# A decode-attention kernel: the last V tile is loaded in five pieces and multiplied slot by slot into small accumulators

## The chip, the cores and the metric

The kernel runs on one core of one Trainium2 chip. The metric is the time of one execution on the device, in microseconds (us). Executions of one kernel that belong together agree within about 0.3%, so a difference of less than one per cent needs several runs of both kernels on the same chip. "Before" and "after" are the two kernels.

Names used throughout: PE is the matmul engine, PEld its weight loads, DVE the vector engine, ACT the scalar engine, SP the engine that issues most loads. A "landing" is the moment at which the semaphore of a load is complete.

## The reference, cut to what matters

One query token attends to 65,536 keys: 32 query heads in 8 groups, one key/value head per group, head size 128.

```python
B, Hq, Hkv, Sq, Sk, D = 1, 32, 8, 1, 65536, 128      # bf16
k = jnp.repeat(k, Hq // Hkv, axis=1)                  # 4 query heads share a K/V head
v = jnp.repeat(v, Hq // Hkv, axis=1)
scores = jnp.einsum("bhqd,bhkd->bhqk", q, k) * D ** -0.5
p = softmax(scores, axis=-1)
return jnp.einsum("bhqk,bhkd->bhqd", p, v)
```

K and V together are 268 MB and each byte is used once, so the least that any kernel can do is to read them.

## The kernel before

K and V of a group are each read as four tiles of 4 MB (128 partitions of 32 KB; 128 "slots" of 128 values on each partition). Loads go through five buffers, one load for each tile. K tiles of group g+1 alternate with V tiles of group g, so the last four loads of the program are V tiles of group 7.

```python
def load(view, name):
    t = iopool.tile([P, T * D], bf16, name=name, tag="io")      # T = 128 slots, D = 128
    nc.sync.dma_start(out=t[:, :], in_=view)
    return t
# ... k_step: scores of a K tile into S;  softmax: S -> E (bf16 weights of V) and rl (1/sum)

def v_step(g, j):                                   # V tile j of group g
    vt = load(v_view[g, j], "vt")
    if j == 0:
        A_tiles[g] = psa.tile([P, 2, HI * D], fp32, name="A")   # two PSUM banks
    A, E = A_tiles[g], E_tiles[g]
    vt_v = vt[:, :].rearrange("p (u i c d) -> p u c i d", u=2, i=HI, c=CW)
    for c0 in range(0, CW, NQ):
        for u in range(2):
            for s in range(NQ):                     # four groups of 32 output partitions
                c = c0 + s
                nc.tensor.matmul(out=A[s * QP:(s + 1) * QP, u, :],
                    lhsT=E[:, j, c, :], rhs=vt_v[:, u, c, :, :],
                    start=(j == 0 and c0 == 0), stop=(j == NQ - 1 and c0 == CW - NQ))

def finish(g):
    A = A_tiles.pop(g)
    As = apool.tile([P, 2, HI, D], fp32, name="As")
    nc.scalar.copy(out=As[:, 0, :, :].rearrange("p i d -> p (i d)"), in_=A[:, 0, :])
    nc.vector.tensor_copy(out=As[:, 1, :, :].rearrange("p i d -> p (i d)"), in_=A[:, 1, :])
    ps_f = psm.tile([HPG, D], fp32, name="ps_f", tag="misc")
    for i in range(NI):                             # 8 matmuls select the useful blocks of As
        nc.tensor.matmul(out=ps_f[:, :], lhsT=sel[:, i * HPG:(i + 1) * HPG],
            rhs=As[:, i // HI, i % HI, :], start=(i == 0), stop=(i == NI - 1))
    o = stats.tile([HPG, D], bf16, name="o")
    nc.vector.tensor_scalar_mul(out=o[:, :], in0=ps_f[:, :], scalar1=rl_tiles.pop(g)[:, :])
    nc.scalar.dma_start(out=out[0, g * HPG:(g + 1) * HPG, 0, :], in_=o[:, :])
# ... cut
```

A matmul of `v_step` multiplies 32 columns of weights by 512 columns of V, of which only a block diagonal is wanted. That saves instructions; `finish` picks the wanted blocks, copied to `As`, with the 8 matmuls of `ps_f`. In the profile these are 16 passes, since an fp32 matmul shows as two.

Of the kernel before, what the change touches and what calls it, by code (L numbers as in the profile page):

```python
# [12 lines left out]
fp32 = mybir.dt.float32  # L13
# [5 lines left out]
def kernel(  # L19
# [19 lines left out]
    nc = tc.nc  # L39
    P = nc.NUM_PARTITIONS  # L40
    B, Hq, Sq, D = q.shape
    _, Hkv, Sk, _ = k.shape
    HPG = Hq // Hkv
    assert B == 1 and Sq == 1 and D == P and HPG == 4 and Hq == 32
    NQ = 4
    QP = 32
    T = Sk // (NQ * NQ * QP)
    NI = QP // HPG
    CW = T // NI
# [9 lines left out]
    apool = ctx.enter_context(tc.tile_pool(name="apool", bufs=1))  # L59
    stats = ctx.enter_context(tc.tile_pool(name="stats", bufs=2))  # L60
    pss = ctx.enter_context(tc.tile_pool(name="pss", bufs=1, space=bass.MemoryType.PSUM))
    psa = ctx.enter_context(tc.tile_pool(name="psa", bufs=1, space=bass.MemoryType.PSUM))
    psm = ctx.enter_context(tc.tile_pool(name="psm", bufs=2, space=bass.MemoryType.PSUM))

    k_view = k[0].rearrange("g (j p t) d -> g j p (t d)", j=NQ, p=P)
    v_view = v[0].rearrange("g (j p t) d -> g j p (t d)", j=NQ, p=P)

    def load(view, name):
        t = iopool.tile([P, T * D], bf16, name=name, tag="io")
        nc.sync.dma_start(out=t[:, :], in_=view)  # L70
        return t

    q4 = const.tile([P, D], bf16)
# [4 lines left out]
    for g in range(Hkv):  # L78
# [9 lines left out]
        out=sel[:, :], in_=ident[:, :].rearrange("p (s c) -> p c s", s=NQ),  # L88
        axis=AX.X, op=ALU.add,
    )  # L90
    selh = const.tile([P, HPG], fp32)
    nc.vector.tensor_reduce(
        out=selh[:, :], in_=sel[:, :].rearrange("p (i h) -> p h i", h=HPG),
# [11 lines left out]
    for a in range(NQ):  # L105
        r = slice(a * QP, (a + 1) * QP)
        z0 = QP - HPG + a * QP
        for b in range(2):
            for e in range(2):
                nc.vector.tensor_copy(  # L110
                    out=Z[r, b, e, :, z0:z0 + HPG], in_=qT_v[r, b, e, :, :]
# [3 lines left out]
    E_tiles = {}  # L115
    rl_tiles = {}
    A_tiles = {}

    def k_step(g, j):
        kt = load(k_view[g, j], "kt")  # L120
        if j == 0:
            S_tiles[g] = pss.tile([P, NQ, 512], fp32, name="S")
        S = S_tiles[g]
        for i in range(NI):
            kT = ktp.tile([P, CW * D], bf16, name="kT")
            nc.vector.transpose(  # L126
                out=kT[:, :].bitcast(i32),
                in_=kt[:, i * CW * D:(i + 1) * CW * D].bitcast(i32),
            )
            kT_v = kT[:, :].rearrange("q (c b p e) -> q b e c p", b=2, p=QP, e=2)  # L130
            for be in range(4):
                b, e = be // 2, be % 2
                w0 = QP - HPG - i * HPG
                nc.tensor.matmul(  # L134
                    out=S[:, j, :NCOL],
                    lhsT=Z[:, b, e, g, w0:w0 + P],
                    rhs=kT_v[:, b, e, :, :],
                    start=(i == 0 and be == 0),
                    stop=(i == NI - 1 and be == 3),
                )  # L140

    def softmax(g):
        S = S_tiles.pop(g)
        mx = stats.tile([P, 1], fp32, name="mx")
        nc.vector.reduce_max(out=mx[:, :], in_=S[:, :, :NCOL], axis=AX.XY)  # L145
        ps_t = psm.tile([1, P], fp32, name="ps_t", tag="misc")
        nc.tensor.transpose(out=ps_t[:, :], in_=mx[:, :], identity=ident[:, :])  # L147
        m4 = stats.tile([1, HPG], fp32, name="m4")
        nc.vector.tensor_reduce(
            out=m4[:, :], in_=ps_t[:, :].rearrange("o (r h) -> o h r", h=HPG),  # L150
            axis=AX.X, op=ALU.max,
        )
        mrow = stats.tile([1, P], fp32, name="mrow")
        nc.vector.tensor_scalar_mul(  # L154
            out=mrow[:, :].rearrange("o (r h) -> o r h", h=HPG),
            in0=m4[:, None, :].to_broadcast([1, P // HPG, HPG]),
            scalar1=-SCALE,
        )
        ps_b = psm.tile([P, 1], fp32, name="ps_b", tag="misc")
        nc.tensor.matmul(out=ps_b[:, :], lhsT=mrow[:, :], rhs=one[:, :], start=True, stop=True)  # L160
        nm = stats.tile([P, 1], fp32, name="nm")
        nc.vector.tensor_copy(out=nm[:, :], in_=ps_b[:, :])  # L162
        ET = etp.tile([P, NQ * NCOL], bf16, name="ET")
        ls = stats.tile([P, 1], fp32, name="ls")
        nc.scalar.activation(  # L165
            out=ET[:, :].rearrange("p (a n) -> p a n", a=NQ), in_=S[:, :, :NCOL],
            func=ACT.Exp, bias=nm[:, :], scale=SCALE, accum_out=ls[:, :],
        )
        E = epool.tile([P, NQ, CW, QP], bf16, name="E")
        nc.vector.transpose(out=E[:, :, :, :].rearrange("p a c r -> p (a c r)"), in_=ET[:, :])  # L170
        E_tiles[g] = E
        ps_l = psm.tile([HPG, 1], fp32, name="ps_l", tag="misc")
        nc.tensor.matmul(out=ps_l[:, :], lhsT=selh[:, :], rhs=ls[:, :], start=True, stop=True)  # L173
        rl = stats.tile([HPG, 1], fp32, name="rl")
        nc.vector.reciprocal(out=rl[:, :], in_=ps_l[:, :])
        rl_tiles[g] = rl

    HI = NI // 2

    def v_step(g, j):  # L180
        vt = load(v_view[g, j], "vt")
        if j == 0:
            A_tiles[g] = psa.tile([P, 2, HI * D], fp32, name="A")
        A = A_tiles[g]
        E = E_tiles[g]
        vt_v = vt[:, :].rearrange("p (u i c d) -> p u c i d", u=2, i=HI, c=CW)
        for c0 in range(0, CW, NQ):
            for u in range(2):
                for s in range(NQ):
                    c = c0 + s  # L190
                    nc.tensor.matmul(  # L191
                        out=A[s * QP:(s + 1) * QP, u, :],
                        lhsT=E[:, j, c, :],
                        rhs=vt_v[:, u, c, :, :],
                        start=(j == 0 and c0 == 0),
                        stop=(j == NQ - 1 and c0 == CW - NQ),
                    )

    def finish(g):
        A = A_tiles.pop(g)  # L200
        E_tiles.pop(g)
        As = apool.tile([P, 2, HI, D], fp32, name="As")
        nc.scalar.copy(out=As[:, 0, :, :].rearrange("p i d -> p (i d)"), in_=A[:, 0, :])  # L203
        nc.vector.tensor_copy(out=As[:, 1, :, :].rearrange("p i d -> p (i d)"), in_=A[:, 1, :])  # L204
        ps_f = psm.tile([HPG, D], fp32, name="ps_f", tag="misc")
        for i in range(NI):
            nc.tensor.matmul(  # L207
                out=ps_f[:, :], lhsT=sel[:, i * HPG:(i + 1) * HPG],
                rhs=As[:, i // HI, i % HI, :],
                start=(i == 0), stop=(i == NI - 1),  # L210
            )
        o = stats.tile([HPG, D], bf16, name="o")
        nc.vector.tensor_scalar_mul(out=o[:, :], in0=ps_f[:, :], scalar1=rl_tiles.pop(g)[:, :])  # L213
        nc.scalar.dma_start(out=out[0, g * HPG:(g + 1) * HPG, 0, :], in_=o[:, :])

    for kind, g, s in seq:
        if kind == "k":
            k_step(g, s)
            if s == NQ - 1:
                softmax(g)  # L220
        else:
            v_step(g, s)
            if s == NQ - 1:
                finish(g)


# [28 lines left out]
```

## Time and profile before

| | before |
|---|---|
| time, median of the first 3 runs | 640.2 us (639.99 to 642.45) |
| read from HBM | 268.5 MB, 420 GB/s over the span of 638.6 us |
| PE, DVE busy | 61%, 54% |
| last landing to the scaling that makes `o` | 629.46 to 635.75: 6.29 us |
| scaling to the end (store, closing drain) | 635.75 to 638.58: 2.83 us |

These are two lines of the page of before. The digits are tenths, one for each of 40 equal slices of the span: the clock that PE was granted, and the busy share of the 16 DMA engines.

```profile
PEclk9998888877688776777767887668886779877767
DMA  8999999999999999999999999999999999999991
```

The reader is to see that the loads never pause until the last slice. Only what follows the last landing counts. The chain of waits of before shows that part in order of time (columns: start, duration, what).

```profile
589.55 39.91 DMA vt<-in_v_dram
629.46 0.04 issue
629.50 3.58 PE A L191 x32
...
633.16 0.59 ACT As L203
633.75 0.04 issue
633.80 1.92 PE ps_f L207 x16
635.72 0.02 issue
635.75 0.34 DVE o L213
```

The 32 matmuls of the last tile, the copies of A and the collecting passes stand one behind another. Windows of before cut this stretch by stage (columns: window; its length; busy time and number of instructions of PE, PEld, DVE, ACT and POOL; granted PE clock; DMA share; GB/s).

```profile
616.00:623.00 7.00, 3.20 (x32) 1.31 (x32) 0.00 (x0) 0.00 (x0) 0.00 (x0) 0.53 0.99 426
623.00:629.46 6.46, 0.09 (x4) 0.00 (x0) 0.00 (x0) 0.00 (x0) 0.00 (x0) 0.74 0.43 183
629.50:633.10 3.60, 3.55 (x32) 1.21 (x31) 0.00 (x0) 0.00 (x0) 0.00 (x0) 0.53 0.00 0
633.80:635.80 2.00, 1.91 (x16) 1.30 (x16) 0.72 (x2) 0.00 (x0) 0.00 (x0) 1.00 0.00 0
```

The clock was 0.53 while the last tile was multiplied and 1.00 while it was collected. The DMA share fell to 0.43 well before the landing, because the 16 engines do not end together: the 16 increments of this load's semaphore come between 624.70 and 629.46.

### The profile page before, as it was taken

Reading aid. Unit: us, or ns where it says so; the run is one execution under the profiler, and the core shown is the slowest. Engines: PE = TensorE matmul, PEld = TensorE weight load, DVE = VectorE, ACT = ScalarE, POOL = GpSimd, SP = SyncE. Lnnn points to the kernel's source line nnn. Section 1 sums busy time; section 2 is a strip of 40 time slices with the busy share of each in tenths; the row PEclk is TensorE's granted clock in tenths of the full one; section 3 lists DMA queues with packets and bytes.
Section 4 is the critical chain, followed back from the end, with each engine's and each line's share of the span. In section 5 each row is a group of like instructions: output and inputs, shape, how many; then the busy total and the mean of one; then the engine's idle time right before and its main releaser. Section 6 shows DMA issues by size and latency. Waiting matters only on the chain.

```text
span 638.6 us, 5252 instructions
## 1 busy us (share of the span) xinstructions
PE 390.7 (61%) x2216; PEld 154.6 (24%) x2216; DVE 343.5 (54%) x340; ACT 21.7 (3%) x25; POOL 4.9 (1%) x7
## 2 busy tenths in 40 slices
PE   0695945776447864487644776547666465775533
PEld 0232312232113321133211232213222122222211
DVE  0999833775336754366553655545555564455300
ACT  0000000000001000010000100001000010000100
POOL 3000000000000000000000000000000000000000
PEclk9998888877688776777767887668886779877767
DMA  8999999999999999999999999999999999999991
GB/s 367 445 434 428 427 426 431 442 431 428 432 426 429 431 436 431 430 433 428 427 431 432 431 433 435 428 427 430 433 431 433 433 430 429 432 431 430 427 436 82
DMA packets 9494, 268.80 MB, mean 421 GB/s; under 512 B 1280, under 2 KB 1280, under 8 KB 1280
## 3 DMA queue, kind: packets, MB, share of 16 engines
q1 hardware_dynamic: 9216, 268.44, 97.8%
q8 instruction: 17, 0.28, 0.2%
q10 hardware_dynamic: 256, 0.04, 0.0%
q14 instruction: 5, 0.04, 0.0%
HBM read 268.47 MB, written 0.01 MB: 420 GB/s over the span
## 4 chain that ended last, share of the span: by engine, by line
DMA 55%; PE 19%; DVE 16%; issue 8%; ACT 2%; ACTq 0%; DVEq 0%
DMA kt<-in_k_dram 46%; PE S L134 13%; DVE kT L126 10%; DMA vt<-in_v_dram 6%; PE A L191 4%; DMA q_85<-in_q_dram 2%; DVE E L170 2%; DVE mx L145 2%; PE ps_f L207 2%; ACT ET L165 2%; DVE As L204 1%; PE ps_b L160 0%; DVE o L213 0%; DVE Z L110 0%; PE ps_t L147 0%
## 5 line engine op out<-in xcount | busy, mean ns | idle before, releaser
L134 PE MATMUL S<-kT,Z 128*128 128x512 bf16 x1024 | 288.5, 441 | 187.5 <-DVE kT L126 184.0
L126 DVE STREAM_TRANSPOSE kT<-kt 128x1024 int32<-128x1024 int32 x256 | 292.2, 1205 | 191.5 <-DMA kt<-in_k_dram 190.9
L134 PEld LDWEIGHTS <-Z 128*128 128x128 bf16 x1024 | 110.3, 108 | 364.5 <-issue 285.0
L191 PE MATMUL A<-vt,E 128*32 128x512 bf16 x1024 | 76.7, 431 | 18.0 <-DMA vt<-in_v_dram 17.9
L191 PEld LDWEIGHTS <-E 128*32 128x32 bf16 x1024 | 28.4, 104 | 57.1 <-issue 40.2
L165 ACT ACTIVATE ET<-S,nm 128x2048 bf16<-128x2048 f32 x8 | 15.7, 1967 | 573.2 <-DVE nm L162 573.2
L207 PE MATMUL ps_f<-As,sel 128*4 128x128 f32 x128 | 22.2, 334 | 12.1 <-DVE As L204 9.4
L170 DVE STREAM_TRANSPOSE E<-ET 128x2048 bf16<-128x2048 bf16 x8 | 18.5, 2311 | 16.3 <-ACT ET L165 16.3
L145 DVE TENSOR_REDUCE mx<-S 128x1 f32<-128x2048 f32 x8 | 18.3, 2291 | 12.6 <-PE S L134 12.6
L204 DVE COPY As<-A 128x512 f32<-128x512 f32 x8 | 5.3, 663 | 31.8 <-ACT As L203 31.8
L207 PEld LDWEIGHTS ps_f<-As,sel 128*4 128x4 f32 x128 | 11.6, 100 | 20.7 <-DVE As L204 11.6
L147 PE MATMUL ps_t<-ident,mx 128*1 128x128 f32 x8 | 2.3, 286 | 16.9 <-DVE mx L145 16.9
L213 DVE TENSOR_SCALAR o<-ps_f,rl 4x128 bf16<-4x128 f32 x8 | 2.7, 338 | 14.1 <-PE ps_f L207 14.1
L100 DVE STREAM_TRANSPOSE qT<-q_85 128x64 int32<-128x64 int32 x1 | 0.2, 245 | 16.1 <-DMA q_85<-in_q_dram 16.1
L173 PE MATMUL ps_l<-ls,selh 128*4 128x1 f32 x16 | 1.5, 165 | 8.2 <-ACT ET L165 8.2
L203 ACT COPY As<-A 128x512 f32<-128x512 f32 x8 | 4.6, 576 | 36.0 <-PE A L191 36.0
L147 PEld LDWEIGHTS ps_t<-ident,mx 128*1 128x1 f32 x8 | 0.6, 79 | 19.5 <-DVE mx L145 16.5
L160 PE MATMUL ps_b<-one,mrow 1*128 1x1 f32 x16 | 3.8, 306 | 2.2 <-DVE mrow L154 2.2
L160 PEld LDWEIGHTS ps_b<-one,mrow 1*128 1x128 f32 x16 | 3.2, 245 | 6.6 <-DVE mrow L154 6.6
L162 DVE COPY nm<-ps_b 128x1 f32<-128x1 f32 x8 | 1.2, 151 | 6.3 <-PE ps_b L160 6.3
L104 POOL MEMSET Z<- 128x4992 bf16 x1 | 4.3, 4262 | 0.0
L173 PEld LDWEIGHTS ps_l<-ls,selh 128*4 128x4 f32 x16 | 0.7, 84 | 12.4 <-ACT ET L165 12.4
(29 smaller groups left out, 10.8 us busy)
## 6 DMA issues: line engine op xcount, KB each, us to landing
kt<-in_k_dram SPq DMA_DIRECT2D x32, 4096.0 KB, 45.4
vt<-in_v_dram SPq DMA_DIRECT2D x32, 4096.0 KB, 39.4
out_dram<-o ACTq DMA_DIRECT2D x8, 1.0 KB
q_85<-in_q_dram ACTq DMA_DIRECT2D x4, 8.0 KB, 6.2
```

The source lines that it names most:

```text
L104: nc.gpsimd.memset(Z[:, :, :, :, :], 0.0)
L126: nc.vector.transpose(out=kT[:, :].bitcast(i32), in_=kt[:, i * CW * D:(i + 1) * CW * D].bitcast(i32),)
L134: nc.tensor.matmul(out=S[:, j, :NCOL], lhsT=Z[:, b, e, g, w0:w0 + P], rhs=kT_v[:, b, e, :, :], start=(i == 0 and be == 0), stop=(i == NI - ...
L145: nc.vector.reduce_max(out=mx[:, :], in_=S[:, :, :NCOL], axis=AX.XY)
L147: nc.tensor.transpose(out=ps_t[:, :], in_=mx[:, :], identity=ident[:, :])
L160: nc.tensor.matmul(out=ps_b[:, :], lhsT=mrow[:, :], rhs=one[:, :], start=True, stop=True)
L165: nc.scalar.activation(out=ET[:, :].rearrange("p (a n) -> p a n", a=NQ), in_=S[:, :, :NCOL], func=ACT.Exp, bias=nm[:, :], scale=SCALE, acc ...
L170: nc.vector.transpose(out=E[:, :, :, :].rearrange("p a c r -> p (a c r)"), in_=ET[:, :])
L191: nc.tensor.matmul(out=A[s * QP:(s + 1) * QP, u, :], lhsT=E[:, j, c, :], rhs=vt_v[:, u, c, :, :], start=(j == 0 and c0 == 0), stop=(j == N ...
L203: nc.scalar.copy(out=As[:, 0, :, :].rearrange("p i d -> p (i d)"), in_=A[:, 0, :])
L204: nc.vector.tensor_copy(out=As[:, 1, :, :].rearrange("p i d -> p (i d)"), in_=A[:, 1, :])
L207: nc.tensor.matmul(out=ps_f[:, :], lhsT=sel[:, i * HPG:(i + 1) * HPG], rhs=As[:, i // HI, i % HI, :], start=(i == 0), stop=(i == NI - 1),)
```

## The change

The intent is to shorten the part behind the last landing. The last tile is loaded in five pieces of 64, 32, 16, 8 and 8 slots. The large accumulators then close one tile earlier and are copied and collected while the last tile loads. The slots of the last tile are multiplied one by one, each only by its own 4 columns of weights, so nothing has to be picked afterwards: 120 slots in turn into four groups of 4 rows of a small accumulator `Dp`, the last 8 straight into `ps_f`. A last matmul adds the sum of the four groups. In passing, A and As become two tiles each in all groups, and the last store is issued from SP.

```diff
-    def load(view, name):
+    def load(view, name, cuts=()):
         t = iopool.tile([P, T * D], bf16, name=name, tag="io")
-        nc.sync.dma_start(out=t[:, :], in_=view)
+        edges = [0, *cuts, T]
+        for lo, hi in zip(edges, edges[1:]):
+            nc.sync.dma_start(out=t[:, lo * D:hi * D], in_=view[:, lo * D:hi * D])
...
+    last_a = NQ - 2
+    CUTS = (T // 2, 3 * T // 4, 7 * T // 8, T - T // 16)
+    EDGE = CUTS[-1]
...                      (v_step: A is two tiles A0, A1; group 7 stops at tile last_a)
-    def finish(g):
+    def collect(g, stop):
...                      (as finish, with As in two tiles; returns ps_f, left open if not stop)
+    def last_step(g, j):
+        vt = load(v_view[g, j], "vt", CUTS)
+        E = E_tiles.pop(g)
+        Dp = psm.tile([P, D], fp32, name="Dp", tag="misc")
+        nc.vector.memset(Dp[:, :], 0.0)
+        def slot(t, dst, start, stop):
+            i, c = t // CW, t % CW
+            nc.tensor.matmul(
+                out=dst, lhsT=E[:, j, c, i * HPG:(i + 1) * HPG],
+                rhs=vt[:, t * D:(t + 1) * D], start=start, stop=stop,
+            )
+        ps_f = collect(g, False)
+        for t in range(EDGE):
+            s = t % NQ
+            slot(t, Dp[s * QP:s * QP + HPG, :], t < NQ, t >= EDGE - NQ)
+        Ds = stats.tile([P, D], fp32, name="Ds")
+        nc.vector.tensor_copy(out=Ds[:, :], in_=Dp[:, :])
+        for t in range(EDGE, T):
+            slot(t, ps_f[:, :], False, False)
+        nc.tensor.matmul(
+            out=ps_f[:, :], lhsT=selh[:, :], rhs=Ds[:, :], start=False, stop=True
+        )
+        store(g, ps_f, nc.sync)
```

More of the change, by code (lines that the diff above doesn't have):

```diff
@@ L182, in v_step @@
         if j == 0:
-            A_tiles[g] = psa.tile([P, 2, HI * D], fp32, name="A")
+            A_tiles[g] = [
+                psa.tile([P, HI * D], fp32, name=f"A{u}") for u in range(2)
+            ]
         A = A_tiles[g]
         E = E_tiles[g]
+        end = NQ - 1 if g < Hkv - 1 else last_a
         vt_v = vt[:, :].rearrange("p (u i c d) -> p u c i d", u=2, i=HI, c=CW)
@@ L191, in v_step @@
                     nc.tensor.matmul(
-                        out=A[s * QP:(s + 1) * QP, u, :],
+                        out=A[u][s * QP:(s + 1) * QP, :],
                         lhsT=E[:, j, c, :],
@@ L195, in v_step @@
                         start=(j == 0 and c0 == 0),
-                        stop=(j == NQ - 1 and c0 == CW - NQ),
+                        stop=(j == end and c0 == CW - NQ),
                     )
-    def finish(g):
+    def collect(g, stop):
         A = A_tiles.pop(g)
-        E_tiles.pop(g)
-        As = apool.tile([P, 2, HI, D], fp32, name="As")
-        nc.scalar.copy(out=As[:, 0, :, :].rearrange("p i d -> p (i d)"), in_=A[:, 0, :])
-        nc.vector.tensor_copy(out=As[:, 1, :, :].rearrange("p i d -> p (i d)"), in_=A[:, 1, :])
+        As = [apool.tile([P, HI, D], fp32, name=f"As{u}") for u in range(2)]
+        nc.scalar.copy(out=As[0][:, :, :].rearrange("p i d -> p (i d)"), in_=A[0][:, :])
+        nc.vector.tensor_copy(out=As[1][:, :, :].rearrange("p i d -> p (i d)"), in_=A[1][:, :])
         ps_f = psm.tile([HPG, D], fp32, name="ps_f", tag="misc")
@@ L208, in finish, with store @@
                 out=ps_f[:, :], lhsT=sel[:, i * HPG:(i + 1) * HPG],
-                rhs=As[:, i // HI, i % HI, :],
-                start=(i == 0), stop=(i == NI - 1),
-            )
+                rhs=As[i // HI][:, i % HI, :],
+                start=(i == 0), stop=(stop and i == NI - 1),
+            )
+        return ps_f
+    def store(g, ps_f, dma):
         o = stats.tile([HPG, D], bf16, name="o")
         nc.vector.tensor_scalar_mul(out=o[:, :], in0=ps_f[:, :], scalar1=rl_tiles.pop(g)[:, :])
-        nc.scalar.dma_start(out=out[0, g * HPG:(g + 1) * HPG, 0, :], in_=o[:, :])
+        dma.dma_start(out=out[0, g * HPG:(g + 1) * HPG, 0, :], in_=o[:, :])
+    def last_step(g, j):
[21 more added lines that the diff above has]
+        store(g, ps_f, nc.sync)
     for kind, g, s in seq:
@@ L221 @@
         else:
-            v_step(g, s)
-            if s == NQ - 1:
-                finish(g)
+            if g == Hkv - 1 and s == NQ - 1:
+                last_step(g, s)
+            else:
+                v_step(g, s)
+                if s == NQ - 1:
+                    store(g, collect(g, True), nc.scalar)
 _INS = ['q', 'k', 'v']
```

## The prediction

> **What bounds the kernel now.** The loads. The page gives 268 MB at 420 GB/s over 638.6 us; the DMA engines are 0.9 busy up to the last of 40 slices, PE 61% and DVE 54%. It is a stream of 64 loads of 4 MB (about 9.7 us each), then a tail without loads. Only the tail changes. From the timeline and the chain of waits: the last V tile lands at 629.46; 32 matmuls into A to 633.08; ACT copies half of A to 633.75; DVE the other half only after ACT (633.78, 0.69 us); 16 passes of ps_f 633.80 to 635.72; scaling 0.34; the store and the closing drain to 638.6. Tail after the landing: 9.1 us, of which 2.5 us (store, drain) stays.
>
> **What the last load looks like.** The windows of 1 us show the DMA share fall from 1.06 (623-624) to 0.46 (624-626) and 0.16 (627-628). The packet records say why: of the 16 engines seven are done at 624.3-624.9, seven at 627.4-627.8, one at 628.4, the last at 629.05, each with eight 32 KB packets of 1.215 us for the tile. The Trainium skill, "DMA: Bandwidth & Descriptors", section on why a DMA increments its semaphore by 16, says that each engine posts its own increment and only all 16 mean landed; the trace agrees (16 increments, 624.70 to 629.46). So every piece waits for the slowest engine.
>
> **Landings after (estimates from its 9.72 us a tile plus 0.4 us to the increment).** Slots 0-63 at 624.6, to 95 at 627.1, to 111 at 628.4, to 119 at 629.1, the last at 629.8. I add 0.3 us for 32 more packets per engine: 256-byte packets took 15-18 ns where their bytes at the 32 KB rate need 9.5.
>
> **PE after.** The large accumulators close with V tile 2: its landing 619.8, matmuls to 623.1, both copies now side by side (separate tiles) to 623.9, ps_f to 625.6, all under the load. Slots start there. A slot is a 4-column weight load and a 128-column matmul, in rotating groups. Four groups run together in the trace (the next four 427 ns later for 512 columns, or 215 ns at full clock), so 128 columns allow 14-27 ns a slot; the tightest stretch of PE issues one instruction per 23 ns, 46 ns a slot. At 40 ns, slots 0-119 done near 630.4. The last 8 share one group, one after another: about 0.1 us each, as the ps_f passes (109 ns): 631.2. The closing matmul and its drain 0.5: scaling starts at 631.8 instead of 635.75.
>
> **Sum.** Removed 3.6 + 0.7 + 1.9 = 6.2 us after the landing; added 0.3 (packets) + 0.6 (slots left behind) + 0.8 + 0.5 = 2.2. Gain near 4 us at 40 ns a slot, under 2 at 60. I discount to 3.2 us, as one more instruction fetch (17 of 16 KB, each stalling an engine about 1 us) may hit the slowest engine. Earlier groups' parallel copies save nothing, under the load.
>
> Predicted 637.0 us, 80% range 635.0 to 639.3; faster by over 2% 0.01, within 2% 0.98, slower 0.01.
>
> **To check.** Last landing within 1 us of 629.5; A's ps_f passes before 626; slot starts 25-60 ns apart; 1.5 to 2.5 us from last landing to scaling.
>
> **What would make it wrong.** Small pieces load much slower (2 KB runs); slots at 100 ns each, so the gain vanishes; pieces issued late because of a wait on the queue.

## The result, and the profile after

| | before | after |
|---|---|---|
| median of 6 runs each | 640.3 us (639.99 to 642.45) | 635.41 us (635.2 to 635.73) |
| ratio | | 0.9915, 95% interval 0.9899 to 0.9931 |
| span of the profile | 638.6 us | 633.7 us |
| last landing | 629.46 | 630.14 |
| last landing to the scaling | 6.29 us | 0.91 us |
| scaling to the end | 2.83 us | 2.67 us |

Ratios are computed as the mean time of one kernel's fast runs over that of the other's of the same rounds, so they are not quite the ratio of the medians: 0.9915 of 640.2 us is 634.8, the median is 635.41. The mean of before is pulled up by two runs at 642.2 and 642.45. The second of them was among the three runs that the prediction had, and it took no notice of it.

The direction and the place of the gain were right, the size was too small: 3.2 us were predicted, and the medians are 4.9 us apart, the means 5.5. This is the chain of waits of after for the same stretch.

```profile
600.07 30.08 DMA vt<-in_v_dram
630.14 0.04 issue
630.19 0.61 PE ps_f L238 x8
630.79 0.23 PE ps_f L251 x2
631.02 0.03 issue
631.05 0.34 DVE o L225
```

Nothing is left behind the landing but the last eight slots and the closing matmul. Lines of the timeline of after, PE and the copies only (columns: start, duration, engine, line, operation, number; in brackets the idle time before and its releaser), show what went under the load.

```profile
623.52 0.59 ACT L212 COPY As_3087<-A_2977 128x512 f32<-128x512 f32 x1 [24.37 <-PE A_2977 L200]
...
624.16 1.29 PE L216 MATMUL ps_f<-As_3087,sel 128*4 128x128 f32 x8 [0.31 <-ACT As_3087 L212]
...
626.06 1.16 PE L238 MATMUL Dp<-vt,E 128*4 128x128 bf16 x58
627.62 0.62 PE L238 MATMUL Dp<-vt,E 128*4 128x128 bf16 x32 [0.41 <-DMA vt<-in_v_dram]
...
628.88 0.40 PE L238 MATMUL Dp<-vt,E 128*4 128x128 bf16 x16 [0.63 <-DMA vt<-in_v_dram]
...
629.55 0.28 PE L238 MATMUL Dp<-vt,E 128*4 128x128 bf16 x8 [0.28 <-DMA vt<-in_v_dram]
```

Each batch of slots is done before the next piece lands, and PE waits for the load again each time (the brackets). The pace inside a batch, from the starts in the trace, is 16 slots in 0.223 us, 14 ns a slot. The windows of after answer to those of before.

```profile
616.00:623.80 7.80, 3.56 (x32) 1.21 (x31) 0.00 (x0) 0.28 (x1) 0.00 (x0) 0.50 0.95 402
623.80:626.30 2.50, 2.19 (x41) 1.62 (x38) 0.69 (x1) 0.31 (x1) 0.00 (x0) 0.82 0.79 316
626.30:630.14 3.84, 2.21 (x112) 1.65 (x107) 0.26 (x1) 0.00 (x0) 0.00 (x0) 1.00 0.32 122
630.14:631.05 0.91, 0.82 (x10) 0.53 (x9) 0.03 (x1) 0.00 (x0) 0.00 (x0) 1.00 0.00 0
```

In this profile the clock is full when the last piece lands. In before it was half at that moment.

The sum closes on the profiles: 0.69 us later landing, 5.38 us less from landing to scaling, 0.17 us less after it, together 4.86 us against 4.9 us between the spans. The interval from the landing of V tile 2 to the last one is 9.95 us with the pieces and 9.70 without, so 0.25 of the 0.69 belong to the pieces. The other 0.44 stand already at V tile 2 and are not the change's: there two profiles of one and the same kernel differ by as much (620.20 in after, 619.71 in e1).

### The profile page after: what moved, and what is told of

It is laid out like the page before. It is cut to its first block, busy times and chain, and to the rows that moved or that the text cites. A ratio compares the mean times of both kernels' runs of the same rounds, so it can differ in the third digit from the quotient of the medians.

```text
span 633.7 us, 5456 instructions
## 1 busy us (share of the span) xinstructions
PE 376.3 (59%) x2314; PEld 151.0 (24%) x2314; DVE 344.5 (54%) x342; ACT 21.7 (3%) x25; POOL 4.9 (1%) x7
## 4 chain that ended last, share of the span: by engine, by line
DMA 70%; PE 12%; DVE 9%; issue 7%; ACT 1%; ACTq 0%; DVEq 0%
DMA kt<-in_k_dram 56%; DMA vt<-in_v_dram 12%; PE S L136 8%; DVE kT L128 8%; DMA q_85<-in_q_dram 2%; DVE mx L147 1%; PE ps_f L216 1%; ACT ET L167 1%; PE A_1900 L200 0%; PE A_772 L200 0%; PE A_773 L200 0%; PE A_1901 L200 0%; DVE Z L112 0%; PE A_396 L200 0%; ACTq L77 0%
## 5 line engine op out<-in xcount | busy, mean ns | idle before, releaser
L136 PE MATMUL S<-kT,Z 128*128 128x512 bf16 x1024 | 283.9, 429 | 207.8 <-DVE kT L128 200.8
L136 PEld LDWEIGHTS <-Z 128*128 128x128 bf16 x1024 | 108.2, 106 | 381.5 <-issue 300.1
L200 PEld LDWEIGHTS <-E 128*32 128x32 bf16 x992 | 25.1, 100 | 49.4 <-issue 29.6
L200 PE MATMUL A_2977<-vt,E 128*32 128x512 bf16 x48 | 6.8, 544 | 13.6 <-DMA vt<-in_v_dram 13.6
L200 PE MATMUL A_2652<-vt,E 128*32 128x512 bf16 x64 | 8.1, 426 | 0.0
L200 PE MATMUL A_2653<-vt,E 128*32 128x512 bf16 x64 | 7.9, 421 | 0.0
L200 PE MATMUL A_397<-vt,E 128*32 128x512 bf16 x64 | 7.4, 409 | 0.0
L200 PE MATMUL A_396<-vt,E 128*32 128x512 bf16 x64 | 7.4, 401 | 0.0
L200 PE MATMUL A_2276<-vt,E 128*32 128x512 bf16 x64 | 7.0, 382 | 0.2 <-DMA vt<-in_v_dram 0.2
L200 PE MATMUL A_1148<-vt,E 128*32 128x512 bf16 x64 | 6.9, 382 | 0.0
L200 PE MATMUL A_1524<-vt,E 128*32 128x512 bf16 x64 | 6.9, 382 | 0.0
L200 PE MATMUL A_1900<-vt,E 128*32 128x512 bf16 x64 | 6.9, 382 | 0.0
L200 PE MATMUL A_772<-vt,E 128*32 128x512 bf16 x64 | 6.9, 382 | 0.0
L200 PE MATMUL A_2978<-vt,E 128*32 128x512 bf16 x48 | 6.9, 548 | 0.0
```

Source lines behind the costliest of these rows:

```text
L136: nc.tensor.matmul(out=S[:, j, :NCOL], lhsT=Z[:, b, e, g, w0:w0 + P], rhs=kT_v[:, b, e, :, :], start=(i == 0 and be == 0), stop=(i == NI - ...
L200: nc.tensor.matmul(out=A[u][s * QP:(s + 1) * QP, :], lhsT=E[:, j, c, :], rhs=vt_v[:, u, c, :, :], start=(j == 0 and c0 == 0), stop=(j == e ...
```

## The experiments

Two theories stand against each other where the gain is larger than predicted. The first: all of it lies behind the last landing, the slots run faster than the prediction took, and the clock of PE in that stretch counts as well. The rival: part of it came from elsewhere, by chance or from the parallel copies in all eight groups. Fourteen runs were made, e1 and e5 with unaltered kernels; in each the result was correct. Runs of before stood in the same rounds, 50 in all with the six of the table.

### e1: the changed kernel again

No edit. 

> The changed kernel unaltered, as the yardstick of this chip. Tail theory (all of the gain lies behind the last landing, 6.3 us before against 0.9 us after from the last landing to the scaling): 635.4 us, and before at 640.2, or near 642.3 in some runs. Rival (part of the gain is chance: two of six runs of before stood at 642.3, which no cause in the tail explains): the ratio moves clearly with the share of such runs, and the difference of the lower runs is 4.8 us, not 5.4.

Measured: 635.21 us (635.2 to 635.42), ratio 0.9903. Before, in the same rounds, 642.11 us (640.11 to 642.42). Of the 50 runs of before exactly half lie between 639.99 and 640.67 (mean 640.32), the other half between 641.99 and 642.48 (mean 642.19), and none between. After has no such second level in 11 runs (mean 635.35). So the gain is 5.0 us over the lower level of before and 6.8 over the upper, and any ratio depends on how many runs of each level it holds. The rival is right that chance is in the ratio; what makes the levels is the next question.

### e5: the kernel before again, for one more profile

No edit, one run, state unknown. 

> The kernel before, unaltered, for one more profile. It has two levels, about 640.2 and 642.2. Clock theory: at the upper level the 16 passes of the last ps_f run at half clock (213 ns apart, 3.6 us) and not at full clock (109 ns, 1.9 us) as in the profile of 640.5; at the lower level they look as there. Rival (the level comes from the loads, an engine that falls further behind): the upper level shows the last landing near 631.4 and the passes 109 ns apart.

Measured: 642.02 us, so an upper run with a profile. First its windows of the tail, then the collecting passes from its timeline:

```profile
616.00:623.00 7.00, 3.38 (x32) 1.35 (x32) 0.00 (x0) 0.00 (x0) 0.00 (x0) 0.50 1.03 445
623.00:629.30 6.30, 0.23 (x4) 0.00 (x0) 0.00 (x0) 0.00 (x0) 0.00 (x0) 0.50 0.42 182
629.30:633.00 3.70, 3.60 (x32) 1.21 (x31) 0.00 (x0) 0.00 (x0) 0.00 (x0) 0.50 0.00 0
633.60:637.30 3.70, 3.57 (x16) 1.88 (x16) 0.71 (x2) 0.01 (x1) 0.00 (x0) 0.50 0.00 0
```

```profile
633.66 3.57 PE L207 MATMUL ps_f<-As,sel 128*4 128x128 f32 x16 [0.74 <-ACT As L203]
```

The last landing is at 629.28, no later than in the lower run (629.46). The passes take 3.57 us at clock 0.50 where they took 1.91 at 1.00. That is 1.66 of the 1.71 us by which the stretch from landing to scaling is longer here (8.00 against 6.29), and the loads have no part in it. The Trainium skill, "TensorE: Matmul & The Clock Gate", section "Part 1: The HAM clock gate", says that the clock is half by default and is raised after a window of about 3.4 us of sustained matmuls, that windows run free of the kernel, and that it falls again after an idle one. The trace agrees: in the lower run the clock record changes at 605.6, 609.0, 612.4, 615.8, 622.6, 626.1 and 632.9, always by multiples of 3.4 us; in the upper run the windows fall otherwise, and from 607.5 to the end none of them raises the clock. In the lower run the window from 629.5 to 632.9 is filled with matmuls, and the clock rises at its end. In the upper run edges lie near 628.0, 631.4, 634.8 and 638.2 (an estimate: 607.51 plus multiples of 3.41 us), so each window of the tail holds a wait of PE. That the place of the windows makes the level rests on these two profiles and on the next experiment, which moves the clock by hand.

### e6 and e9: the kernel before, with PE kept at work while it waits

```diff
+    def keep_warm(vt):
+        W = psm.tile([P, 512], fp32, name="W", tag="misc")      # never read
+        for n in range(14):                                     # e9: 20
+            nc.tensor.matmul(out=W[:, :], lhsT=vt[:, 0:P], rhs=vt[:, P:P + 512],
+                start=(n == 0), stop=(n == 13))
...                      (in v_step, behind the matmuls of V tile 2 of group 7)
+        if g == Hkv - 1 and j == NQ - 2:
+            keep_warm(vt)
```

> The kernel before with 14 dummy matmuls (128 by 512, into an unread bank) between the multiplication of V tile 2 and that of tile 3, so that PE works while it would have waited for the last load. Nothing leaves the tail. Clock theory: the clock is full when the tile lands, the 32 matmuls take 2.0 us and not 3.6, the collecting passes 1.9 us always: landing to scaling 4.9 us, 638.7 us, and no run near 642. That would be 1.5 us of the gain over the lower level of before and 3.4 over the upper. If the clock doesn't matter: 640.2 and 642.2 as before.

Measured: 638.9 us (638.55 to 640.42), ratio 0.9967; four runs from 638.55 to 639.06, two above 640.1, none near 642. In the profile, of a run at 640.16, the dummies ended at 625.9 and the clock fell to half at 629.1, 0.1 us ahead of the landing. So the wait was still long enough to lose the clock, and the forecast of 638.7 us missed two of the six runs. The edit was made longer:

> As e6_before_warm with 20 dummy matmuls, not 14: there they ended 3.4 us ahead of the landing, and in the profile the clock fell to half just before it. Twenty end 1 to 2.5 us ahead. Clock theory: all runs near 638.6, from landing to scaling 4.9 us, none at 640 or 642. Rival (the runs at 638.6 of e6 had another cause): the same spread, 638.5 to 640.4.

Measured: 638.97 us, all five runs between 638.72 and 638.98. Timeline of e9:

```profile
623.86 4.85 PE L204 MATMUL W<-vt 128*128 128x512 bf16 x19 [0.33 <-issue]
...
629.62 1.91 PE L191 MATMUL A<-vt,E 128*32 128x512 bf16 x32 [0.91 <-DMA vt<-in_v_dram]
...
632.27 1.91 PE L217 MATMUL ps_f<-As,sel 128*4 128x128 f32 x16 [0.74 <-ACT As L213]
```

The same 32 matmuls that took 3.55 us take 1.91. Useless work under the load made the kernel 1.4 us faster than its lower level and 3.3 us faster than its upper one, and both levels vanished. This is the strongest run: it changes the clock and nothing else behind the landing. The clock is thus a part of what the change gains, since it also puts work on PE during the last load. What is left from e9 to after, 638.9 to 635.35, is 3.5 us, and that is work moved from behind the landing.

### e7: only the accumulators and their copies in two tiles

The changed kernel, with its last tile treated as every other one.

```diff
-        end = NQ - 1 if g < Hkv - 1 else last_a
+        end = NQ - 1
...
-            if g == Hkv - 1 and s == NQ - 1:
+            if False:
                 last_step(g, s)
```

> The large accumulators and their copies in two tiles each, in all eight groups, and nothing else of the change. Tail theory: copies of the first seven groups lie under the loads; in the last, ACT can start when its half is done, 0.3 to 0.5 us: between 0 and 0.5 us faster than before, with the two levels of before. Rival (a good part of the gain comes from parallel copies in all groups): 2 us or more faster.

Measured: 640.18 us (640.03 to 640.95), ratio 0.9985, interval 0.9968 to 1.0001. From landing to scaling the profile has 5.92 us, 0.37 less than before, as expected. The rival's 2 us are not there. One part of the forecast failed: none of six runs is at the upper level. In its profile the clock record rises at 633.6, just as the passes begin. Whether six lower runs are luck (one chance in 64, if half the runs were upper) or the earlier start of the passes helps the clock was not settled.

### e10: only the five pieces

The kernel before, its last tile loaded with the five cuts, and multiplied as before.

```diff
-        vt = load(v_view[g, j], "vt")
+        vt = load(v_view[g, j], "vt", CUTS if g == Hkv - 1 and j == NQ - 1 else ())
```

> The kernel before with its last V tile loaded in five pieces, the rest as it was: what the pieces cost by themselves. By the landings of the changed kernel (9.95 us from V tile 2 to the last piece, where one load took 9.70) the pieces cost 0.25 us; the first four matmuls can start earlier, which saves at most 0.4 us. So 640.0 to 640.5 at the lower level, 642.0 to 642.5 at the upper. If small pieces load much slower: 641 or more at the lower level and an interval from V tile 2 to the last landing above 10.5 us.

Measured: 640.33 us; three runs from 639.53 to 639.70, three from 640.96 to 641.3. The interval from V tile 2 to the last landing is 9.94 us, as expected, so small pieces load nearly as fast as one large one. The forecast of the total missed: it had the levels of before unchanged, and both are lower, by 0.7 and 1.1 us. In the profile the matmuls behind the first four begin at 628.99, half a microsecond before the last landing at 629.49, since 16 of these 28 need only the first four pieces.

### e2: the last tile in one load

```diff
-        vt = load(v_view[g, j], "vt", CUTS)
+        vt = load(v_view[g, j], "vt")
```

> The last V tile in one load; small accumulators and early collection stay. Slot theory (four column groups overlap, 14 ns a slot): 120 slots after the landing cost 1.7 us, the copy of the small accumulators and its waits about 0.6 us more, less 0.25 us for the landing that no longer carries 32 extra packets an engine: from landing to scaling 2.6 to 3.2 us, total 1.6 to 2.2 us above the changed kernel, about 637.3. With the 40 ns a slot of the prediction: 120 slots cost 4.8 us and the total is 640 or more, no better than before.

Measured: 638.53 us (636.7 to 639.36), ratio 0.9951. Timeline of its profile, a run at 639.36:

```profile
629.85 3.37 PE L238 MATMUL Dp<-vt,E 128*4 128x128 bf16 x120 [3.37 <-DMA vt<-in_v_dram]
```

The 120 slots took 3.37 us, 27 ns each, at a clock of 0.50 in the window from 629.7 to 632: again PE had been idle for 3.4 us. The forecast, made at full clock, was 1.2 us too low at the median; the fastest run, 636.7, is near it. At 40 ns a slot no run could have been that fast. So the pieces are worth about 3.2 us to this design, of which the pace of the slots at full clock explains about half.

### e3: all slots into one group of four rows

```diff
-            s = t % NQ
-            slot(t, Dp[s * QP:s * QP + HPG, :], t < NQ, t >= EDGE - NQ)
+            slot(t, Dp[0:HPG, :], t == 0, t == EDGE - 1)
```

> All 120 slots go to one group of four partitions instead of four in turn. Slot theory (the 14 ns come from the overlap of four groups): the slots run at about 55 ns, as the last eight did, 6.6 us for 120; PE then falls behind the load, ends slot 119 near 632.5 and scaling starts near 633.4, 2.3 us later than in the changed kernel: about 637.7. Rival (issue of two instructions a slot sets the pace, not the groups): the slots stay at the same pace and the time does not move from 635.4.

Measured: 637.95 us (637.64 to 638.56), 2.6 us above after. Timeline of e3:

```profile
625.88 6.86 PE L238 MATMUL Dp<-vt,E 128*4 128x128 bf16 x120
632.58 0.61 PE L238 MATMUL ps_f<-vt,E 128*4 128x128 bf16 x8
```

The slots now start every 56 ns without a pause, and scaling starts at 633.54, 2.5 us later than in after. The pace of 14 ns comes from the overlap of four groups; the issue of two instructions a slot does not limit it. The overlap is what the Trainium skill describes in "TensorE: Matmul & The Clock Gate", section "Part 3: Packing small matmuls": matmuls whose outputs lie in different strips of 32 partitions run at the same time. The trace agrees: 56 ns for one, 56 ns for four.

### e11: every slot multiplied twice

```diff
-            slot(t, Dp[s * QP:s * QP + HPG, :], t < NQ, t >= EDGE - NQ)
+            slot(t, Dp[s * QP:s * QP + HPG, :], t < NQ, False)
+            slot(t, Dp[s * QP:s * QP + HPG, :], False, t >= EDGE - NQ)
...
-        nc.vector.tensor_copy(out=Ds[:, :], in_=Dp[:, :])
+        nc.vector.tensor_scalar_mul(out=Ds[:, :], in0=Dp[:, :], scalar1=0.5)
```

> Each of the 120 slots multiplied twice, the sum halved in the copy of the small accumulators, so the result is right. Slot theory: 28 ns for a slot of the tile at full clock against 76 ns that its load takes, so all but the 8 doubled matmuls of the fourth piece stays hidden: 0 to 0.2 us above the changed kernel, 635.2 to 635.6. With the 40 ns of the prediction, 80 ns for a slot of the tile: PE would end slot 119 near 635 and the time would be 640.

Measured: 636.33 us (636.14 to 636.44), 1.0 us above after: a miss for the forecast of 0 to 0.2, and far from the 640 of a 40 ns pace. Timeline of e11:

```profile
625.53 3.18 PE L238 MATMUL Dp<-vt,E 128*4 128x128 bf16 x200
...
630.25 0.66 PE L238 MATMUL Dp<-vt,E 128*4 128x128 bf16 x33 [1.53 <-issue]
```

Two hundred matmuls in 3.18 us is the same pace of 14 to 16 ns. Then PE stood still for 1.53 us with the third and the fourth piece landed (628.28 and 628.95) and nothing that the profile shows to wait for. The record of the instruction queue has a fetch of 16 KB from 627.83 to 628.94, the 18th of the run. By its time the pause may be a wait for instructions, but this is argued and not shown: PE began again only 1.3 us after the end of that fetch, and in after a fetch from 628.78 to 630.08 stands beside no such pause. The pace of the slots stands; the price of doubling them is this pause, and its cause stays open.

### e4 and e8: collecting the large accumulators late

```diff
-        ps_f = collect(g, False)
         for t in range(EDGE):
...
+        ps_f = collect(g, False)        # e4: moved here, behind the 120 slots
```

> The 8 matmuls that collect the large accumulators (16 passes, 1.9 us) are put behind slot 119 instead of ahead of slot 0. Tail theory: they run only when the fourth piece has been multiplied, 629.7 to 631.4, and push the last eight slots: 1.2 to 1.5 us more than the changed kernel, about 636.8. If early collection were worth nothing: 635.4.

Measured: 635.32 us (635.09 to 635.66), no different from after. The run says nothing: in its timeline the collecting matmuls run ahead of the slots as before (from 623.90, the first slot at 626.15). A moved line is not a moved instruction. For e8 a dependence was added that enforces the order:

```diff
+        selw = stats.tile([P, QP], fp32, name="selw")
+        nc.vector.scalar_tensor_tensor(out=selw[:, :], in0=Ds[:, :QP], scalar=0.0,
+            in1=sel[:, :], op0=ALU.mult, op1=ALU.add)
+        ps_f = collect(g, False, selw)  # behind the copy to Ds
```

> Collection of the large accumulators behind slot 119, this time enforced: its selection matrix is made from the copy of the small accumulators (times zero, plus the old matrix), so PE cannot run it earlier; the order of the compiled instructions shows it there. Tail theory: 16 passes at full clock, 1.75 us, and the little operation on DVE, 0.2 us, move behind the last landing: scaling 1.7 to 2.2 us later than in the changed kernel, about 637.3. If early collection were worth nothing: 635.3.

Measured: 639.29 us (638.33 to 639.58), 4 us above after and not 2. In the profile the clock is 0.50 from 607.65 to 634.96 and the 16 passes take 3.57 us. So collecting early is worth what it takes away and, in this profile, the clock. That the clock stays low because PE has less to do under the load is argued and not shown.

### e12: large accumulators kept, the tile in two halves

The last tile is loaded in two pieces, the matmuls go over one accumulator and then the other, and the first is copied and collected under the second piece.

```diff
+        vt = load(v_view[g, j], "vt", (T // 2,))
+        for u in range(2):
...                      (16 matmuls into A[u]; copy A[u] to As on DVE; 4 matmuls into ps_f)
```

> A rival design without small accumulators: last tile in two halves, the half of the columns of each large accumulator that is complete is copied and collected while the second half loads. What is left behind the last landing: 16 of the 32 matmuls, one copy on DVE, 8 of the 16 passes: 2.9 us to the scaling at full clock, 4.6 at half clock, against 6.3 or 8.0 of before and 0.9 of the changed kernel. So 637.0 to 639.0. If the small accumulators and early collection were no better than this: 635.4.

Measured: 638.94 us (638.14 to 639.1), ratio 0.9964. From landing (629.44) to scaling (634.08) 4.64 us, at half clock, as expected. Small accumulators with early collection are 3.6 us better than this simpler design.

### e13: three small loads behind the last piece

```diff
+        pr = const.tile([8, D], bf16, name="pr")
+        for n in (1, 7, 8):
+            nc.sync.dma_start(out=pr[0:n, :], in_=v[0, 0, 0:n, :])
```

> The changed kernel with three small loads of 1, 7 and 8 partitions queued behind the last piece, for the times at which single engines come to the end of their queue. Theory (the instruction fetches, each beside one step back of one engine's landings, hit the same engines each time, the others never): the loads of 1 and 7 partitions land 3 us or more ahead of the last piece, that of 8 does too or has one late part. Rival (any engine may be hit): late parts among the first 7. The time doesn't matter here; it should stay within 0.5 us of 635.3.

Measured: 636.03 us, one run of unknown state, 0.7 us above after where 0.5 were allowed. The load of 7 partitions was issued only near 625.9, and that of 8 was scheduled behind the store, so they did not see the end of the queue as meant. Still, the seven parts landed at 626.6 to 626.8 (four), 628.1, 628.3 and 629.2, where the parts of the last piece landed at 625.0 to 625.6 (seven), 627.9 to 628.5 (seven), 629.0 and 629.8. So three of the seven parts of this load are late too, as the rival had it. Giving some engines a larger share of the last tile, which would have been the next version to try, has no basis in this run.

### e14: the last store from ACT

```diff
-        store(g, ps_f, nc.sync)
+        store(g, ps_f, nc.scalar)
```

> The changed kernel with its last store issued from ACT, as before, and not from SP. From the start of the scaling to the end of the span before took 2.83 us (ACT) and after 2.65 (SP): 0.2 us slower than the changed kernel, 635.5. If the issuing engine doesn't matter: 635.3.

Measured: 635.24 us (634.89 to 636.12); in the profile 2.64 us from scaling to end, after has 2.67. The issuing engine does not matter here. The 0.17 us by which this stretch was longer in the profile of before stay unexplained; over the profiles it is 2.36 (e8) to 2.94 us (e2), both stored from SP.

The profile shows something else. It is of a run at 635.78, and its clock fell to half at 629.25, before the last landing at 629.74:

```profile
629.70:632.00 2.30, 1.44 (x10) 0.93 (x9) 0.43 (x2) 0.00 (x0) 0.00 (x0) 0.50 0.00 0
```

From landing to scaling it took 1.52 us, not 0.91. So the changed tail can lose the clock too, but with so little work left there it costs 0.6 us and not 1.7.

No experiment points to a version that beats after by more than its runs scatter, so none was made. What is left behind its last landing is 0.9 us of work and 2.67 us of store and drain.

## Why the prediction was right or wrong

**Right: what bounds the kernel and where the gain lies.** The loads run as before, the change works behind the last landing, 6.2 us were said to leave it and 6.29 us stood there. The rival causes were tried alone: the split tiles take 0.4 us from this stretch (e7), the engine of the store nothing (e14).

**Right: the pieces.** 0.3 us were predicted, 0.25 measured from landing to landing (0.24 in e10). The last landing was predicted at 629.8 and came at 630.14, of which the 0.44 us that were there already at V tile 2 are scatter from run to run (in e1 the last landing is 629.66).

**Right: slots start at about 625.6** (625.84), with the collecting passes done under the load.

**Wrong, the step that failed first: "At 40 ns, slots 0-119 done near 630.4".** The prediction had the right range, 14 to 27 ns, from the overlap of four groups, and passed it over for the tightest pace of instructions seen in the trace, 23 ns each. After shows that this was no limit: it runs a matmul and a weight load in 14 ns. Measured: 13.9 ns a slot at full clock, 26.7 at half (e2), 56 in one group (e3). No slots were left behind the landing, where 0.6 us were predicted.

**Wrong: "about 0.1 us each" for the last eight.** They started every 55 ns, 0.44 us together instead of 0.8. The figure was taken from fp32 passes at full clock (109 ns); the bf16 matmuls of the same shape took half of that.

**Nearly right: the closing matmul.** 0.5 us predicted, 0.42 measured (630.63 to 631.05). From landing to scaling 2.0 us were predicted and 0.91 measured.

**Wrong, and the largest single term: the discount from 4 to 3.2 us for one more instruction fetch.** The fetch came (18 instead of 17, from 628.78 to 630.08), and it cost the load nothing that can be measured: from V tile 2 to the last landing after took 9.95 us with it, and e10, which has 17 fetches, 9.94. PE does not pause beside it either. Of the four checks, that of the last landing held; the slots started 14 ns apart and not 25 to 60, landing to scaling took 0.91 us and not 1.5 to 2.5, and the passes ended at 626.3, just past 626.

**Missing: the clock.** The windows of before showed 0.53 and 1.00 in the two halves of the tail, and the first three runs had one at 642.45. The prediction read neither. The tail of before runs at a clock that depends on where free-running windows fall: 640.3 or 642.2 us (e5), and 638.9 if PE is kept at work (e9). After has work for PE during the last load, and in its profile and that of e1 the clock was full when the last piece landed (in e14 it was not). Over the lower level the change gains 5.0 us. Of these 1.4 could be had by the clock alone; over the mean of all 50 runs of before, 641.26, it gains 5.9, of which 2.4 by the clock.

With the two sizes of slots right and without the discount, the sum of the prediction would have been 6.2 less 0.3, 0.44 and 0.5, which is 5.0 us: the gain over the lower level. So the mechanism was right and three terms were mis-sized: 0.8 us for the discount, 0.6 for slots left behind and 0.36 for the last eight. The rest, up to the 5.5 us between the means, is the runs of before at the upper level.

**Open:** why e7 had no upper run, why the stretch from scaling to end differs by 0.17 us, and which DMA engine is last. The traces hold a lead on the last: after the first 3 us of before, 22 packets of 32 KB take 1.63 us or more where the median is 1.215, and each of them starts within 0.02 us of the end of one of its 22 instruction fetches. The increments of a load lie within 0.6 us before the first fetch (42.8 us) and 1.8 us apart at 53. That the fetches part the engines is suggested by this and not shown: no run changed them.

## What to carry to other kernels

Before a stretch of small matmuls is costed, ask what limits it: matmuls in turn into four strips of 32 output partitions started every 14 ns here, where one strip took 56, and a pace read elsewhere in the trace is no bound. When an engine waits for the last load, what it does during the wait can set the clock at which it does the rest (1.4 us in e9), so read the granted clock by stage, and look at every run of before, since two levels in its times are a fact about the kernel. After an edit of the order of lines, look at the compiled order before the chip is asked.

## What the Trainium skill lacked or had wrong

- "TensorE: Matmul & The Clock Gate", section "Wait — 56ns, not 53.3ns?", gives about 25 ns as the least start-to-start time of matmuls however small they are. That is too wide: Part 3 of the same page gives about 4 ns for each further tile of a pack. Matmuls of 128 columns in rotating strips of 32 output partitions started every 14 ns on average here, each with its own weight load, 58 of them in a row in after and 200 in e11: in after bursts of four, 3 to 6 ns apart, one burst every 56 ns.
- Part 1 of the same page says that the number of slow matmuls varies from run to run with the place of the windows at the kernel's start. It does not say that a stretch behind the last load can put the runs of one kernel on two levels with nothing between: 640.32 and 642.19 us here, 25 runs each, by whether the clock rose in that stretch.
- "Runtime: NRT & Kernel Launch", section "Instruction fetch mechanics", calls the cost of crossing a 16 KiB block mostly hidden. For the last load that held (9.95 us with such a fetch in after, 9.94 without one in e10). In e11 PE paused for 1.53 us behind such a fetch (627.83 to 628.94); whether the fetch was the cause is not shown. The section has nothing on the loads beside a fetch: in before, at the end of each of the 22, one 32 KB packet of a load took 1.63 us or more, for 1.215.
- "DMA: Bandwidth & Descriptors" says that the 16 engines finish independently and has no figure for how far they part over a long stream. In before the 16 increments of one 4 MB load lay within 0.6 us in the first tiles and within 4.8 us in the last, and the slowest engine sets every landing.
